# Three stores of 128 rows cut into 114 rows and 14 rows in a one-core attention and MLP gradient kernel

## The chip, the core and the metric

The kernel runs on one core of one Trainium2 chip. The metric is the device time of one execution in microseconds (us); lower is better. A core has a matrix engine (TensorE, PE in the profile), VectorE (DVE), ScalarE (ACT), GpSimd (POOL) and SyncE (SP), which issues the data transfers here, and 16 DMA engines that carry them out between device memory and the core's on-chip memory.

## The reference, cut to what matters

The forward pass adds three things: the input `x`, one decode step of grouped-query attention over a long key/value cache, and a gated MLP without a nonlinearity. The kernel computes this output and the gradients of all tensor inputs that carry one, for a given `grad_out`.

```python
# B=2, Sq=1, D=576, Hq=32, Hkv=16, Sk=4096, Dh=128, F=4608, all bf16
xn  = layernorm(x)
q   = (xn @ wq) per head;  k, v = caches repeated to 32 heads
p   = softmax(q k^T / sqrt(Dh));  o = p v;  A = o @ wo
h   = (xn @ w_gate) * (xn @ w_up);  B_ = h @ w_down
out = x + A + B_
out, vjp = jax.vjp(f, x, k_cache, v_cache, wq, wo, w_gate, w_up, w_down)
return (out, *vjp(grad_out))
```

With two rows of input, nearly all bytes are the caches (each 2x16x4096x128) and the weights, which are read once, and their gradients, which have the same shapes and are written once.

## The kernel before, in words

The work is cut into streams. There are 16 attention steps `s` (8 groups of key/value heads times 2 batch rows); each loads two heads of K and two of V, 1 MB each, transposes them, computes scores, softmax and their gradients, and writes two heads of dK and two of dV, 1 MB each. There are 9 MLP slices of 512 columns, and 8 groups for the projections `wq` and `wo`. Every weight slice is loaded, used, and its gradient (an outer product of a short vector pair) is built in PSUM by PE, copied to on-chip memory by ACT or DVE (the helper `cp`, lines 422 and 424) and stored.

All these streams are generators that ask a planner, `Order`, for engines, buffers and transfers. The planner runs once while the program is built and writes one fixed order of instructions for each engine. It does not run on the chip. Transfers are asked for with `DMA("SP", cost, bytes, row)`, and all of them but two small loads at the start are issued by SP (`nc.sync.dma_start`). The compiler's framework gives every transfer one of eight completion counters in turn, so a transfer is issued only once the transfer eight places before it has landed.

The tiles `big` (16 of 1 MB) hold loaded caches, transposed caches, gate and up weights, and results that wait to be stored (`st`). `put` is the stream of a store. It waits until the result is complete, issues the transfer, and hands its buffer back when the transfer has landed:

```python
def put(dst, src, nbytes, row, tag, slot, ready):
    yield WAIT(*ready)
    for d, x in zip(dst, src):
        yield DMA("SP", 0.36, nbytes, row)
        nc.sync.dma_start(d, x)
    yield ("lrel", tag, slot)
```

`rows_outer` uses it for the gradients of `wo` and `w_down`: 17 slices of 512 rows of 576, laid out as 128 partition rows of 4608 bytes (`row` is 4608 for these and no other store). Each slice is 576 KB. The other stores are dK and dV (rows of 8192 bytes, 1 MB), and the gradients of `wq`, `w_gate` and `w_up` (rows of 1024 to 4096 bytes). The two outputs of two rows each (`rows_put`, line 1422) are stored from the tile `xy`; the second of them is the last transfer in SP's list.

Of the kernel before, what the change touches and what calls it, by code (L numbers as in the profile page):

```python
# [232 lines left out]
def WAIT(*events):  # L233
    return ("wait", events)
# [14 lines left out]
def DMA(engine, cost, nbytes, row=8192):  # L249
    return ("dma", engine, cost, 0.01 + RATE * nbytes / 16e3 * (0.03676 + 8.0 / row))  # L250
# [45 lines left out]
    "wo": [-13, -2, -15, 2, 36, -14, 47, 53],  # L296
    "mlp": [2, 16, -13, 39, 111],
}
LATENCY, DRY, RATE = 0.5, 0.9, 1.009
LM, LAG, DRIFT = 0.67, 2.2, 0.009  # L300
CLK = 1.65
# [9 lines left out]
def kernel(  # L311
# [22 lines left out]
    nc = tc.nc  # L334
# [298 lines left out]
    def dxn(dp, Wm, X, S, pos, xoff, blocks):  # L633
        for s in range(S):
            for q in range(4):
                nc.tensor.matmul(dp[32 * q:32 * q + 32, :], lhsT=view(Wm[:], 0, P, 8 * pos(q, s), [[1, 32]]),  # L636
                                 rhs=view(X, 0, P, xoff(q, s), [[FS, blocks], [2, 32]]),
                                 start=(s == 0), stop=(s == S - 1))

    def put(dst, src, nbytes, row, tag, slot, ready):  # L640
        yield WAIT(*ready)
        for d, x in zip(dst, src):
            yield DMA("SP", 0.36, nbytes, row)
            nc.sync.dma_start(d, x)
        yield ("lrel", tag, slot)

    def unit(mms, pe, cols, ev, done, quad=None, kind="r"):
# [34 lines left out]
    def rows_outer(t, dst, p, event):  # L682
        i = yield ACQ("st")
        st, done = st_t[i], events(FC)
        yield SPAWN(put([dst.rearrange("(p c) n -> p (c n)", c=FC)], [st[:, 0:FC * D]], 128 * FC * D * 2, 4608,
                        "st", i, done), p + pr("store"))
        for j in range(FC):
            yield SPAWN(unit(*rows_unit(j, t, st), done[j]), p)
        yield WAIT(*done)
        yield SET(event)  # L690

    def cols_store(i, dst, width, done):
        return put([dst.rearrange("(c p) n -> p c n", p=P)], [st_t[i][:, 0:4 * width].rearrange("p (c n) -> p c n", n=width)],
                   128 * 4 * width * 2, 2 * width, "st", i, done)
# [25 lines left out]
    def wide_outer(rhss, dst, p, event):  # L720
        width, last = FS * len(rhss), []
        for d0 in (0, 2):
            i = yield ACQ("st")
            done = events(4)
            last += done
            yield SPAWN(put([dst[P * d0:P * d0 + 2 * P, :].rearrange("(c p) n -> p c n", p=P)],
                            [st_t[i][:, 0:2 * width].rearrange("p (c n) -> p c n", n=width)],
                            128 * 2 * width * 2, 2 * width, "st", i, done), p + pr("store"))
            for c in range(2):
                for A in range(2):  # L730
                    yield SPAWN(unit(*wide_unit(rhss, d0 + c, A, st_t[i], c * width), done[2 * c + A]), p)
        yield WAIT(*last)
        yield SET(event)
# [800 lines left out]
```

## Time and profile before

| what | value |
|---|---|
| median of 3 runs | 471.64 us (471.35 to 472.25) |
| the profiled execution: its own time, its span | 471.37 us, 469.6 us |
| PE, DVE, ACT, POOL busy, share of the span | 79%, 79%, 71%, 31% |
| bytes moved | 185.96 MB, mean 396 GB/s |
| mean granted clock of TensorE | 0.710 |

The profiled execution lasts 1.8 us longer than its span from first to last instruction. Times in the views count from the start of the span. A row of the table by stretches gives, for each engine, its busy time and in brackets its instructions, then the granted clock, the mean busy share of the 16 DMA engines (1.00 is all of them all the time; packets that follow each other overlap a little, so it can be over 1), and the rate in GB/s. In the view of the transfers over a stretch, the line `DMA` has the same share in 40 equal slices, in tenths, and the line `GB/s` the rate in each.

### The profile page before, as it was taken

The page shows a single profiled execution, that of the slowest core. Times are in us where ns is not written, and L with a number is a line of the kernel's source. Part 1 is how long each engine was busy: PE and PEld are TensorE (multiplying, and loading weights), DVE is VectorE, ACT ScalarE, POOL GpSimd, SP SyncE. Part 2 cuts the span into 40 slices and gives each one's busy share as a digit, 9 for nine tenths or more (in the row PEclk, how much of TensorE's full clock was granted, in tenths as well). Part 3 has the DMA queues.
Part 4 walks back from the last instruction along what each step waited for, and adds up shares of the span by engine and source line. Part 5 has one row for each costly group of instructions (what it writes and reads, how often), then busy time and mean ns, then how long its engine had stood idle before and what let it go on. Part 6 is the DMA issues. An engine that isn't in the chain of part 4 may idle for free.

```text
span 469.6 us, 15459 instructions
## 1 busy us (share of the span) xinstructions
PE 370.8 (79%) x6636; PEld 217.5 (46%) x6636; DVE 369.5 (79%) x705; ACT 334.3 (71%) x507; POOL 146.8 (31%) x176
## 2 busy tenths in 40 slices
PE   0588688869887777986997669789699898998984
PEld 0455444435653352554463444564345434444453
DVE  9689878967867879688689658978867978898772
ACT  2149668867885948671798638877678678789973
POOL 3350242681330320203252264000843705325100
PEclk9978897767757668776675767956656658566977
DMA  8999999999999999999999999999999989999995
GB/s 317 404 413 403 363 390 419 409 416 421 418 416 420 399 421 406 412 415 419 399 418 404 386 418 424 408 413 342 413 416 393 424 270 416 423 413 413 424 368 176
DMA packets 40053, 185.96 MB, mean 396 GB/s; under 512 B 3496, under 2 KB 11184, under 8 KB 23600
## 3 DMA queue, kind: packets, MB, share of 16 engines
q1 hardware_dynamic: 39976, 184.96, 98.1%
q8 instruction: 52, 0.85, 0.7%
q14 instruction: 17, 0.14, 0.1%
q10 hardware_dynamic: 8, 0.00, 0.0%
HBM read 92.48 MB, written 92.48 MB: 394 GB/s over the span
## 4 chain that ended last, share of the span: by engine, by line
PE 42%; ACT 18%; DVE 18%; DMA 12%; issue 5%; POOL 2%; SPq 2%; ACTq 0%; DVEq 0%; POOLq 0%
ACT big L422 15%; DMA out_dram<-big 10%; DVE big L418 8%; PE ps_m L1378 8%; PE ps_o L1226 7%; PE ps_m L1205 7%; PE ps_o L675 4%; PE ps_m L841 3%; DVE big L424 3%; DMA big<-in_A_v_cache_dram 3%; PE ps_m L967 2%; PE ps_m L636 2%; POOL BD L1193 2%; PE ps_o L712 1%; SPq L1129 1%
## 5 line engine op out<-in xcount | busy, mean ns | idle before, releaser
L422 ACT CAST big<-ps_o 128x1024 bf16<-128x1024 f32 (+4 forms) x319 | 279.7, 950 | 40.3 <-PE ps_o L1226 18.2
L418 DVE STREAM_TRANSPOSE big<-big 128x1024 f32<-128x1024 f32 x146 | 176.1, 1223 | 5.9 <-DMA big<-in_A_v_cache_dram 3.6
L1193 POOL TENSOR_TENSOR BD<-vr,mask 128x2048 bf16<-128x2048 bf16 x32 | 115.2, 3603 | 198.8 <-ACT vr L422 122.2
L424 DVE CAST big<-ps_o 128x1024 bf16<-128x1024 f32 (+2 forms) x71 | 78.2, 1102 | 15.8 <-PE ps_o L675 5.2
L1205 PE MATMUL ps_m<-big,W 128*32 128x128 bf16 x2048 | 57.1, 274 | 5.5 <-ACT osb L422 0.7
L1226 PE MATMUL ps_o<-BD,dd 32*128 32x512 bf16 x256 | 48.8, 489 | 12.7 <-ACT big L422 9.2
L1205 PEld LDWEIGHTS <-W 128*32 128x32 bf16 x2048 | 45.4, 121 | 21.9 <-issue 18.6
L1226 PE MATMUL ps_o<-BD,pp 32*128 32x512 bf16 x256 | 42.1, 461 | 10.4 <-ACT big L422 6.7
L1170 POOL COPY W<-rep 32x16 bf16<-32x16 bf16 x128 | 24.5, 192 | 63.5 <-DVE rep L951 53.2
L418 DVE STREAM_TRANSPOSE big<-ww 128x1152 f32<-128x1152 f32 (+1 forms) x25 | 32.9, 1317 | 4.5 <-DMA out_dram<-big 3.3
L1378 PE MATMUL ps_m<-big,pp 128*32 128x512 bf16 x256 | 28.2, 536 | 1.5 <-DVE small L1330 1.2
L1378 PE MATMUL ps_m<-big,dd 128*32 128x512 bf16 x256 | 27.5, 518 | 1.5 <-DVE dd L418 0.6
L1226 PEld LDWEIGHTS <-dd 32*128 32x128 bf16 x256 | 11.8, 97 | 32.4 <-issue 24.7
L1226 PEld LDWEIGHTS <-pp 32*128 32x128 bf16 x256 | 10.4, 95 | 26.9 <-issue 22.6
L422 ACT CAST osb<-ps_m 128x512 bf16<-128x512 f32 x15 | 8.9, 590 | 15.9 <-PE ps_m L1378 12.6
L675 PE MATMUL ps_o<-dyr,R 32*32 32x288 bf16 x256 | 17.3, 402 | 2.0 <-ACT big L422 2.0
L675 PE MATMUL ps_o<-dyr,hb 32*32 32x288 bf16 x288 | 16.5, 346 | 1.1 <-ACT big L422 0.9
L967 PE MATMUL ps_m<-big,Wdy 128*128 128x128 bf16 x144 | 14.9, 285 | 3.1 <-DVE small L1283 2.0
L712 PEld LDWEIGHTS <-xnr 32*128 32x128 bf16 x368 | 12.5, 119 | 9.3 <-issue 8.6
L422 ACT CAST sp<-ps_m 128x256 bf16<-128x256 f32 x22 | 8.4, 380 | 11.2 <-PE ps_m L1213 11.0
L636 PEld LDWEIGHTS <-wm 128*32 128x32 bf16 x704 | 13.4, 115 | 6.3 <-issue 5.1
L841 PE MATMUL ps_m<-big,Wdy 128*128 128x128 bf16 x162 | 15.6, 272 | 0.6 <-DVE small L1291 0.4
(210 smaller groups left out, 481.9 us busy)
## 6 DMA issues: line engine op xcount, KB each, us to landing
out_dram<-big SPq DMA_DIRECT2D x74, 1024.0 KB, 12.1
big<-in_A_k_cache_dram SPq DMA_DIRECT2D x32, 1024.0 KB, 12.4
big<-in_A_v_cache_dram SPq DMA_DIRECT2D x32, 1024.0 KB, 12.5
out_dram<-big SPq DMA_DIRECT2D x17, 576.0 KB, 11.4
ww<-in_B_w_down_dram SPq DMA_DIRECT2D x9, 576.0 KB, 11.1
ww<-in_A_wo_dram SPq DMA_DIRECT2D x8, 576.0 KB, 11.1
ww<-in_A_wq_dram SPq DMA_DIRECT2D x8, 512.0 KB, 11.6
big<-in_B_w_gate_dram SPq DMA_DIRECT2D x4, 1024.0 KB, 13.1
```

The source lines that it names most:

```text
L418: nc.vector.transpose(out, in_)
L422: nc.scalar.copy(out, in_)
L424: nc.vector.tensor_copy(out=out, in_=in_)
L636: nc.tensor.matmul(dp[32 * q:32 * q + 32, :], lhsT=view(Wm[:], 0, P, 8 * pos(q, s), [[1, 32]]), rhs=view(X, 0, P, xoff(q, s), [[FS, blocks ...
L675: nc.tensor.matmul(o[32 * q:32 * q + 32, aa, 0:HD2], lhsT=view(t, 32 * q, 32, 2 * A + aa, [[4, 32]]), rhs=dyr[32 * q:32 * q + 32, k * HD2: ...
L841: nc.tensor.matmul(dh, lhsT=Wdy[:, e, 2 * k:2 * k + P], rhs=view(X[:], 0, P, 64 * k + e, [[D, FC], [2, 32]]), start=(k == 0 and e == 0), s ...
L967: nc.tensor.matmul(dp, lhsT=Wdy[:, e, 2 * k:2 * k + P], rhs=view(X[:], 0, P, 64 * k + e, [[D, GH], [2, 32]]), start=(k == 0 and e == 0), s ...
L1170: nc.gpsimd.tensor_copy(view(W_t[t][w][:], 32 * a, 32, 6 + 8 * a, [[G * WW, 4], [WW, G], [1, 2]]), view(rep_t[grp[g]["qs"]][:], 32 * a, 32 ...
L1193: nc.gpsimd.tensor_tensor(BD_t[i][:], view(vr_t[v][:], 0, P, 0, [[0, 16], [1, Dh]]), view(mask16[:], 0, P, 0, [[1, 16], [0, Dh]]), ALU.mult)
L1205: nc.tensor.matmul(sc[32 * cq:32 * cq + 32, :], lhsT=view(W[:], 0, P, (be * G + l) * WW + 6 - 4 * c2 - 2 * l, [[1, 32]]), rhs=view(X[:], 0 ...
L1226: nc.tensor.matmul(o[:, k, :], lhsT=pr2[32 * c4:32 * c4 + 32, :], rhs=BD[32 * c4:32 * c4 + 32, 8 * l + 4 * h2:8 * l + 4 * h2 + 4, :], star ...
L1378: nc.tensor.matmul(ct[32 * j:32 * j + 32, :], lhsT=view(rT, 0, P, 4 * c + 2 * l, [[1, 32]]), rhs=kv_t[kvS[s][t][l]][:, Dh * c:Dh * (c + 4) ...
```

## The change

A list `stores` counts the stores with rows of 4608 bytes in the order in which the planner issues them. The 9th, 13th and 15th of the 17 are issued as two transfers, the first 114 partition rows and then the last 14. The planner is asked for one transfer, as before, so its order and its costs are what they were.

```diff
+PARTS, CUT = (114, 14), (9, 13, 15)
...
+    stores = []
+
+    def parted(d, x, parts):
+        if parts is None:
+            nc.sync.dma_start(d, x)
+            return
+        r = 0
+        for n in parts:
+            nc.sync.dma_start(d[r:r + n], x[r:r + n])
+            r += n
+
     def put(dst, src, nbytes, row, tag, slot, ready):
         yield WAIT(*ready)
         for d, x in zip(dst, src):
             yield DMA("SP", 0.36, nbytes, row)
-            nc.sync.dma_start(d, x)
+            if row == 4608:
+                stores.append(slot)
+            parted(d, x, PARTS if row == 4608 and len(stores) in CUT else None)
         yield ("lrel", tag, slot)
```

PE, ACT, DVE and POOL keep their instructions in the same order. SP's list has three transfers more. From the first cut on every transfer takes the next of the eight counters instead of its old one, so it waits for another transfer than before.

## The prediction

> **What bounds the kernel now.** I read the page first, then the stretches of time, then the transfers of the last 5 us, then the waits of SP and the chain.
>
> ```profile
> span 469.6 us, 15459 instructions
> ...
> PE 370.8 (79%) x6636; PEld 217.5 (46%) x6636; DVE 369.5 (79%) x705; ACT 334.3 (71%) x507; POOL 146.8 (31%) x176
> ...
> DMA packets 40053, 185.96 MB, mean 396 GB/s; under 512 B 3496, under 2 KB 11184, under 8 KB 23600
> ...
> q1 hardware_dynamic: 39976, 184.96, 98.1%
> ...
> PE 42%; ACT 18%; DVE 18%; DMA 12%; issue 5%; POOL 2%; SPq 2%; ACTq 0%; DVEq 0%; POOLq 0%
> ```
>
> The 16 DMA engines are busy 98.1% of the span with SP's queue, the compute engines 79% at most. The chain nevertheless puts only 12% on transfers, since it walks back through compute wherever a buffer came free in time. So transfers set the pace, with compute close behind. A mean over 16 engines hides whether they finish together. The end of the span shows that they don't. This is the view of the transfers from 464.4 to 469.6 us, 0.13 us a slice:
>
> ```profile
> DMA  9999998311111000000000000000000000000000
> GB/s 351 366 347 339 331 347 284 97 47 47 47 47 47 32 24 24 24 24 24 24 24 24 24 24 32 24 24 16 24 0 0 0 0 0 0 0 0 0 0 0
> ```
>
> Fourteen engines are done at about 465.4 us. Two go on until 466.1 us (47 GB/s), and one alone until 468.2 us (24 GB/s). So one engine is late: 2.7 us behind fourteen others and 2.0 us behind the second. The kernel's end waits for it. It was late 10 us earlier too. From 457.2 to 458.8 us, SP's queue shows just one engine's worth of packets:
>
> ```profile
> q1 hardware_dynamic: 10, 0.04, 7.5%
> ```
>
> One engine of 16 is 6.25%, and 0.04 MB in 1.6 us is 25 GB/s. While the others had nothing left, this one still worked off its backlog. A transfer has landed only when its last engine is done, so each landing that compute waits for comes when the late engine gets there. The stretches show where the others run dry:
>
> ```profile
> core 0: us, PE busy (x) PEld busy (x) DVE busy (x) ACT busy (x) POOL busy (x), PEclk, DMA share, GB/s
> 100.00:110.00 10.00, 7.36 (x103) 5.17 (x103) 4.48 (x11) 3.70 (x8) 5.96 (x6) 0.50 1.01 423
> 250.00:262.00 12.00, 9.52 (x171) 5.15 (x170) 11.57 (x16) 8.43 (x13) 4.37 (x5) 0.63 0.96 380
> 317.00:330.00 13.00, 11.53 (x209) 5.34 (x212) 10.86 (x19) 9.18 (x14) 0.27 (x1) 0.63 0.96 345
> 345.00:416.00 71.00, 64.41 (x921) 32.78 (x921) 56.98 (x106) 54.35 (x82) 27.02 (x40) 0.62 0.98 391
> 375.00:380.00 5.00, 4.75 (x60) 2.19 (x58) 4.41 (x8) 3.50 (x5) 0.02 (x1) 0.50 0.59 204
> 410.00:415.00 5.00, 5.00 (x104) 3.40 (x108) 3.95 (x7) 4.09 (x7) 0.00 (x0) 0.50 1.02 428
> 455.00:464.00 9.00, 7.29 (x190) 5.13 (x190) 4.92 (x19) 6.40 (x10) 0.00 (x0) 0.88 0.66 235
> ```
>
> With all 16 at work the share is 1.02 (410 to 415). What a row lacks to 1.02, times its length, is the mean idle time of an engine: 0.7 us at 250, 0.8 at 317, 2.8 from 345 to 416 (2.15 of it in the dip from 375 to 380), 3.2 at 455. That is cover for extra work on any engine but the late one.
>
> **How the rows fall on the engines.** SP issues 218 transfers of 64 or 128 rows and two of two rows, ACT two of two rows. The page has 3496 packets under 512 B, and no row of data is that short: 218 x 16 + 4 x 2 = 3496. Each transfer thus ends with one small packet on each engine that it uses: 16 engines for 64 and 128 rows, two for two rows. An equal share per engine fits all three. Carried on, 114 = 6 x 19 uses 6 engines with 19 rows each, and 14 rows use 14 engines with one each. I take these as the same end of the row of engines each time. Then a cut store puts 20 rows on six engines, 1 on eight and 0 on two, where each had 8.
>
> The Trainium skill ("DMA: Bandwidth & Descriptors", "Why a DMA increments its semaphore by 16 and not by 1") gives the rule outright: the largest number up to 16 that divides both sides' row counts, lowest-numbered engines first. The trace agrees for 2, 64 and 128 rows; nothing run so far shows 114.
>
> **The price of a row.** 423 GB/s over 16 engines (100 to 110) is 26.4 GB/s for one, so 4608 bytes take 0.175 us. A cut adds 12 rows or 2.1 us to each of the six, takes 7 rows or 1.2 us from eight, 8 rows or 1.4 us from two. Three cuts: +6.3 us on six, -3.7 and -4.2 us on the rest.
>
> **Where the cuts lie.** SP's timeline, and the size line of the transfers:
>
> ```profile
> 201.69 9.38 SPq L644 DMA_DIRECT2D out_dram<-big  x4
> ...
> 333.61 0.35 SPq L644 DMA_DIRECT2D out_dram<-big  x1
> ...
> 406.66 5.61 SPq L644 DMA_DIRECT2D out_dram<-big  x2
> ```
>
> ```profile
> out_dram<-big SPq DMA_DIRECT2D x17, 576.0 KB, 11.4
> ```
>
> In SP's list the 9th of the 17 is the last of the four at 201.69, the 13th is alone at 333.61, the 15th is the second of the two at 406.66. Issued at about 211, 334 and 412, they land 11.4 us later, at about 222, 345 and 423.
>
> **Is the late engine one of the six?** The end of SP's own wait tells something:
>
> ```profile
> SPq L644 <- ACT big L422: 112.3, 58, 6.9
> ...
> SPq L1087 <- DMA out_dram<-big: 16.0, 10, 3.4
> ...
> SPq L1529 <- DMA out_dram<-big: 3.5, 1, 3.5
> ```
>
> The last wait of the program (L1529) ends with a store of `big`, although the two-row store of `xy` is the last in SP's list. The two engines of that store were done before the late one. If two-row transfers use two of the six, the late engine is one of 14, and four of these are in the six: 4/14, or 0.29, that it is hit, 10/14 that it is relieved. I forecast that it is relieved.
>
> The Trainium skill ("DMA: Bandwidth & Descriptors", "Latency and other measured facts") calls engines 7 and 15 usually slower in traces. With its rule of lowest numbers neither is among the six, which would raise the chance; a view of before doesn't name the engine.
>
> **The sum.** The late engine loses 7 or 8 rows three times: 3.7 to 4.2 us less work, and it has no idle time to lose them in. At the end, fourteen others stand 2.7 us ahead of it and the second latest 2.0 us. If nothing upstream moves, the end comes earlier by 2.0 to 2.7 us. Upstream, three pieces of the chain after the first cut are landings:
>
> ```profile
> 257.52 12.04 DMA big<-in_A_v_cache_dram
> ...
> 300.09 16.17 DMA out_dram<-big
> ...
> 423.19 6.32 DMA out_dram<-big
> ```
>
> The first can end 1.2 us sooner. The third begins just behind the third cut; it can end sooner by 2.4 us (the second and the third cut on the late engine), or later by up to 2.1 us (what the six hold more). So the whole lies between 4.2 us gained and nothing. I take 2.2 us, since the end is shown by rows and the upstream share isn't.
>
> The six: +2.1 us at 222 meet 1.5 us of idle time before 345 (250 and 317), which leaves 0.6. With the next 2.1 they are 2.7 behind and meet 2.8 us (345 to 416), all covered. The last 2.1 meet 3.2 us (455). So they shouldn't end last. Without that cover they would be up to 6.3 us behind.
>
> The smaller edits:
>
> ```profile
> L644 SPq DMA_DIRECT2D out_dram<-big x105: 332/344/2885, 35.3 to 463.5; - x105
> ...
>   ACT big L422: 5.8, 2
>   DVE big L418: 4.3, 3
> ```
>
> Three more issues at 0.34 us are 1.0 us on SP, which waits 112.3 us for ACT's copies. I take zero; at most 1.0 if loads queue behind. The two parts use two of the eight counters, so loads behind them wait for a more recent transfer. Such waits cost 16.0 us in 10 times, 1.6 each. I take zero, since a landing comes some 12 us after its issue and the engines still have work queued; at most 1.6 a cut. A cut store gives its buffer back up to 2.1 us later on the six. ACT and DVE waited 5.8 and 4.3 us in all for buffers of stores, in five places; none is sure to be one of these. Zero to 2.1 us, counted in the range.
>
> The profiled execution took 471.37 us, its span 469.6 us; the median is 471.64 us. 471.37 - 2.2 = 469.2 on the profiled execution, 469.4 us on the median. This case's own range is 467.4 (4.2 gained) to 470.7 us (0.9 gained).
>
> **The rivals.** *The late engine is one of the six.* Then it gets 36 rows more, 6.3 us, and it has no idle time. Every landing that compute waits for comes later, from the first cut on: 471.6 + 6.3 = 477.9 us, and about 475 if half of it falls into stretches where compute sets the pace, as in the dip from 375 to 380. For: 4 of 14 places. Against: 10 of 14. This decides with the first cut: from 222 us on, each landing would be 2.1 us later.
>
> *The six become the late ones.* If their own lateness adds to 2.1 us where the chain waits at 423, that wait ends up to 2.1 us later, and what the end gives is used up: 471.6 to 473.7 us. For it speaks that dips are means over engines, and one of the six can have less. Against it speaks their sum, 7.5 us from 250 to 464 against 6.3 us.
>
> The Trainium skill's rule to use all 16 engines ("DMA: Bandwidth & Descriptors", "Rules for kernel authors") speaks for this rival; no run so far shows it.
>
> *The rows are spread over all engines anyway*, in shares of 7 and 8. Then only three issues are added: 471.7 us.
>
> **How the numbers follow.** A measurement of this kernel can tell about 0.2%, 0.9 us, from no change. Relieved late engine: 0.57 (0.53 faster by more than that, 0.04 within). Late engine hit: 0.27, slower. Six become late: 0.11 (0.03 within, 0.08 slower). Spread anyway: 0.05 (0.04 within, 0.01 slower). Faster 0.53, same 0.11, slower 0.36. The time is that of the likeliest, 469.4 us. The range goes from 467.0 (4.2 us gained, and the runs' own spread of 0.3) to 478.0 us, which takes in the middle of the second case; its upper half stays outside.
>
> **What would show it.** If right, the last 5 us of the changed kernel show the tail of one engine at 24 GB/s shorter than 0.7 us or gone, the 14-row parts are issued right behind the 114-row parts, and the packets under 512 B number 3496 - 48 + 60 = 3508. If instead the tail of one engine grows by several us and dips like those at 375 and 455 get deeper, it was hit. If several engines share a tail of some 2 us, the six are the late ones. If the small packets number 3496 + 48 = 3544, the rows were spread over 16 and the price is wrong.

## The result, and the profile after

| kernel | median us | range, runs |
|---|---|---|
| before | 471.94 | 471.35 to 473.14, 4 |
| three stores as 114 and 14 rows | 478.86 | 477.18 to 479.69, 4 |

The ratio is 1.0144, with a 95% interval from 1.0123 to 1.0165: 6.8 us slower (0.0144 x 471.94). The forecast was 469.4 us. The first rival, "the late engine is one of the six", had 477.9 us. The profiled execution after took 479.12 us with a span of 477.3 us.

The page after, the lines that answer to those of before:

```profile
span 477.3 us, 15459 instructions
...
PE 368.8 (77%) x6636; PEld 215.9 (45%) x6636; DVE 369.6 (77%) x705; ACT 335.1 (70%) x507; POOL 147.1 (31%) x176
...
DMA packets 40065, 185.96 MB, mean 390 GB/s; under 512 B 3508, under 2 KB 11196, under 8 KB 23612
...
q1 hardware_dynamic: 39988, 184.96, 97.5%
...
PE 32%; DMA 26%; DVE 18%; ACT 13%; issue 6%; POOL 2%; SPq 0%; DVEq 0%; ACTq 0%; POOLq 0%
```

Compute has the same busy times (PE 368.8 after 370.8 us, ACT 335.1 after 334.3), so nothing was added there. The share of transfers in the chain went from 12% to 26%; what this share is worth is said with the run of two halves below. The small packets are 3508, as foreseen for six and fourteen engines. The parts were issued one right behind the other in two of the three places; in the second, the two issues took 3.13 us together. This is SP's timeline after:

```profile
212.94 0.85 SPq L651 DMA_DIRECT2D out_dram<-big  x2
...
337.08 3.13 SPq L651 DMA_DIRECT2D out_dram<-big  x2
...
415.50 0.79 SPq L651 DMA_DIRECT2D out_dram<-big  x2
```

The chain after, its transfers from 200 us on:

```profile
208.56 15.10 DMA out_dram<-big
224.06 14.89 DMA ww<-in_A_wo_dram
261.33 11.84 DMA big<-in_A_v_cache_dram
303.81 15.78 DMA out_dram<-big
351.81 13.75 DMA out_dram<-big
403.57 15.14 DMA out_dram<-big
418.79 14.55 DMA big<-in_A_v_cache_dram
```

Before, three transfers stood there with 34.5 us together (12.04, 16.17, 6.32). After, seven stand there with 101.1 us. Two of the four new ones lie near the first cut, but they don't show what it did: the store was issued at 208.56, ahead of the parts (212.94), and the chain of a run that is faster than before (lo4 below) has a landing of 15.26 us at 231.88 too. The rival was to decide with the first cut. That it costs anything is shown by the run with one cut below.

The stretches after, and the last 8 us (0.2 us a slice):

```profile
core 0: us, PE busy (x) PEld busy (x) DVE busy (x) ACT busy (x) POOL busy (x), PEclk, DMA share, GB/s
250.00:262.00 12.00, 9.13 (x118) 4.65 (x121) 10.60 (x16) 10.53 (x15) 2.95 (x10) 0.50 0.91 376
375.00:380.00 5.00, 4.50 (x90) 2.64 (x82) 4.24 (x10) 2.44 (x4) 3.52 (x1) 0.50 1.02 422
422.00:440.00 18.00, 14.48 (x199) 6.32 (x197) 13.98 (x23) 16.85 (x25) 9.41 (x3) 0.62 0.87 307
400.00:477.30 77.30, 61.69 (x984) 33.10 (x983) 53.63 (x102) 57.99 (x84) 16.78 (x9) 0.65 0.89 350
```

```profile
DMA  9997400689999986513711000000000000000000
GB/s 335 356 333 256 149 26 15 236 317 361 346 335 335 361 289 225 179 51 123 251 63 36 20 26 26 20 26 26 26 20 26 26 20 21 0 0 0 0 0 0
```

From 400 us to the end the share was 0.91 before and is 0.89 over a longer time: (1.02 - 0.89) x 77.3 is 10.0 us of mean idle time, against 7.7 us before. The end still is one engine alone with 20 to 26 GB/s, from 473.7 to 476.1 us. That is 2.4 us, little more than the 2.1 us of before. At 470.3 us the same picture shows in the middle of work: 15 to 26 GB/s, one engine.

### The profile page after: what moved, and what is told of

The parts are those of the page before. It is cut to its first block, busy times and chain, and to the rows that moved or that the text cites. A ratio compares the mean times of both kernels' runs of the same rounds, so it can differ in the third digit from the quotient of the medians.

```text
span 477.3 us, 15459 instructions
## 1 busy us (share of the span) xinstructions
PE 368.8 (77%) x6636; PEld 215.9 (45%) x6636; DVE 369.6 (77%) x705; ACT 335.1 (70%) x507; POOL 147.1 (31%) x176
## 2 busy tenths in 40 slices
DMA packets 40065, 185.96 MB, mean 390 GB/s; under 512 B 3508, under 2 KB 11196, under 8 KB 23612
## 4 chain that ended last, share of the span: by engine, by line
PE 32%; DMA 26%; DVE 18%; ACT 13%; issue 6%; POOL 2%; SPq 0%; DVEq 0%; ACTq 0%; POOLq 0%
DMA out_dram<-big 18%; ACT big L425 11%; DVE big L421 9%; DMA big<-in_A_v_cache_dram 6%; PE ps_o L1242 5%; PE ps_m L1221 5%; PE ps_m L1394 5%; DMA ww<-in_A_wo_dram 3%; DVE big L427 3%; PE ps_m L983 3%; PE ps_m L857 2%; PE ps_o L691 2%; POOL BD L1209 2%; PE ps_m L639 1%; PE ps_o L728 1%
## 5 line engine op out<-in xcount | busy, mean ns | idle before, releaser
L1242 PE MATMUL ps_o<-BD,dd 32*128 32x512 bf16 x256 | 48.5, 486 | 15.2 <-ACT big L425 10.8
L1394 PE MATMUL ps_m<-big,pp 128*32 128x512 bf16 x256 | 29.2, 554 | 1.1 <-DVE small L1346 0.7
L691 PE MATMUL ps_o<-dyr,R 32*32 32x288 bf16 x256 | 16.1, 376 | 1.5 <-ACT big L425 1.5
L691 PE MATMUL ps_o<-dyr,hb 32*32 32x288 bf16 x288 | 16.2, 338 | 1.2 <-ACT big L425 1.1
L983 PEld LDWEIGHTS <-Wdy 128*128 128x128 bf16 x144 | 14.2, 134 | 5.6 <-issue 5.6
## 6 DMA issues: line engine op xcount, KB each, us to landing
out_dram<-big SPq DMA_DIRECT2D x74, 1024.0 KB, 13.9
```

What stands on the lines that cost most here:

```text
L691: nc.tensor.matmul(o[32 * q:32 * q + 32, aa, 0:HD2], lhsT=view(t, 32 * q, 32, 2 * A + aa, [[4, 32]]), rhs=dyr[32 * q:32 * q + 32, k * HD2: ...
L983: nc.tensor.matmul(dp, lhsT=Wdy[:, e, 2 * k:2 * k + P], rhs=view(X[:], 0, P, 64 * k + e, [[D, GH], [2, 32]]), start=(k == 0 and e == 0), s ...
L1242: nc.tensor.matmul(o[:, k, :], lhsT=pr2[32 * c4:32 * c4 + 32, :], rhs=BD[32 * c4:32 * c4 + 32, 8 * l + 4 * h2:8 * l + 4 * h2 + 4, :], star ...
L1394: nc.tensor.matmul(ct[32 * j:32 * j + 32, :], lhsT=view(rT, 0, P, 4 * c + 2 * l, [[1, 32]]), rhs=kv_t[kvS[s][t][l]][:, Dh * c:Dh * (c + 4) ...
```

## The experiments

Engines are numbered 0 to 15 here in the order in which transfers of few rows take them. The Trainium skill ("DMA: Bandwidth & Descriptors", "Why a DMA increments its semaphore by 16 and not by 1") has them taken from the lowest number up. The packets of these runs show how many engines each part uses; the number itself no row names. The runs lo2 to lo5 were measured on one chip, the runs from half to lo4x6 on a second one, the last five on two more. On which chip the result above was measured isn't known.

Three explanations were set against each other. A: one engine was late all along, it is one of the six, and it pays 12 rows a cut. B: overloaded engines cost what their overload is, whichever they are. C: the three added transfers cost it, with their issues and counters.

All runs up to the last five change one line, the parts and the stores that are cut. The result of each is given as a ratio to the kernel before on the same chip; below 1 is faster:

| run | parts | stores cut | rows a cut (8 when whole): fullest engines; number 4 | median us | ratio, interval |
|---|---|---|---|---|---|
| lo2 | 34, 80, 14 | 9, 13, 15 | 0 and 1: 23; 6 | 471.97 | 1.0005 (0.9989 to 1.0020) |
| lo3 | 51, 64, 13 | 9, 13, 15 | 0 to 2: 22; 5 | 471.92 | 1.0006 (0.9984 to 1.0028) |
| lo4 | 68, 48, 12 | 9, 13, 15 | 0 to 3: 21; 4 | 470.32 | 0.9967 (0.9951 to 0.9984) |
| lo5 | 85, 32, 11 | 9, 13, 15 | 0 to 4: 20; 20 | 478.35 | 1.0136 (1.0104 to 1.0168) |
| half | 64, 64 | 9, 13, 15 | all: 8; 8 | 472.12 | 1.0006 (0.9989 to 1.0023) |
| one | 114, 14 | 9 | 0 to 5: 20; 20 | 473.70 | 1.0041 (1.0024 to 1.0058) |
| six | 114, 14 | 5, 7, 9, 11, 13, 15 | 0 to 5: 20; 20 | 485.88 | 1.0295 (1.0275 to 1.0316) |
| p120 | 120, 8 | 9, 13, 15 | 0 to 7: 9; 9 | 472.83 | 1.0017 (0.9998 to 1.0036) |
| r2 | 68, 60 | 9, 13 | 0 to 3: 21; 4 | 470.79 | 0.9981 (0.9964 to 0.9998) |
| r3 | 68, 60 | 9, 13, 15 | 0 to 3: 21; 4 | 469.66 | 0.9950 (0.9929 to 0.9970) |
| r3e | 68, 60 | 3, 6, 9 | 0 to 3: 21; 4 | 473.07 | 1.0017 (0.9993 to 1.0041) |
| lo4x6 | 68, 48, 12 | 5, 7, 9, 11, 13, 15 | 0 to 3: 21; 4 | 477.22 | 1.0102 (1.0066 to 1.0138) |

**Which engine: two, three, four or five of them loaded.**

```diff
-PARTS, CUT = (114, 14), (9, 13, 15)
+PARTS, CUT = (34, 80, 14), (9, 13, 15)    # lo2
+PARTS, CUT = (51, 64, 13), (9, 13, 15)    # lo3
+PARTS, CUT = (68, 48, 12), (9, 13, 15)    # lo4
+PARTS, CUT = (85, 32, 11), (9, 13, 15)    # lo5
```

> The same three stores as 34, 80 and 14 rows: 34 rows use two engines with 17 rows each, 80 rows all 16 with 5, 14 rows fourteen with 1. Engines 0 and 1 so carry 23 rows of each cut store (8 before the change), 2 to 13 carry 6, the last two 5. Theory A (one engine was late all along, it is one of the six that the 114-row part uses, but neither 0 nor 1, since a store on two engines alone landed ahead of it): the late engine loses 2 rows a cut, 1.1 us in three; the two loaded ones get 45 rows or 7.9 us more, of which some 4 to 7 us are what they stand ahead of the late one: 471 to 475 us. Theory B (any engines that are overloaded cost what the overload is): 471.9 + 7.9 = 479.8 us. Theory C (it is the added transfers, their issues and counters, not the rows): six more transfers instead of three, twice the 6.9 us of the change: about 486 us.

> The same three stores as 51, 64 and 13 rows: engines 0 to 2 carry 22 rows of each cut store, 3 to 12 carry 5, the last three 4. A: if the late engine is 2, it gets 42 rows or 7.4 us more: 479 us and about the time of the change or over; if it is 3, 4 or 5, it loses 9 rows (1.6 us): 470 to 474 us. B: 471.9 + 7.4 = 479 us, whichever engine is late. C: about 486 us.

> The same three stores as 68, 48 and 12 rows: engines 0 to 3 carry 21 rows of each cut store, 4 to 11 carry 4, the last four 3. A: if the late engine is 2 or 3, it gets 39 rows or 6.8 us more: 479 us; if it is 4 or 5, it loses 12 rows (2.1 us): 470 to 473 us. B: 471.9 + 6.8 = 479 us. C: about 486 us.

> The same three stores as 85, 32 and 11 rows: engines 0 to 4 carry 20 rows of each cut store, 5 to 10 carry 3, the last five 2. A: if the late engine is 2, 3 or 4, it gets 36 rows or 6.3 us more, as in the change: 478 to 479 us; if it is 5, it loses 15 rows (2.6 us): 469 to 473 us. B: 471.9 + 6.3 = 478 us. C: about 486 us. The four runs together: under A there is one step up of 4 to 8 us, at the first of them whose loaded engines include the late one; under B all four are at 478 to 480; under C all four lie above the change.

Two and three loaded engines: no change that could be measured. Four: 1.6 us faster (0.0033 x 471.35). Five: 6.4 us slower. There is one step, between four and five. The step is not one of size, since the fullest engines get 39 rows too many with four of them and 36 with five. Under A the late engine is the fifth to get rows, number 4. B and C fail on the first three runs: 45, 42 and 39 rows too many on other engines and six added transfers cost nothing. From the page the packets, and from the stretches the one with the first cut in it (200 to 300 us), first of the run with four, then of the run with five:

```profile
DMA packets 40101, 185.96 MB, mean 398 GB/s; under 512 B 3544, under 2 KB 11232, under 8 KB 23648
```

```profile
200.00:300.00 100.00, 81.58 (x1437) 49.59 (x1433) 79.58 (x139) 70.04 (x110) 32.09 (x41) 0.68 1.01 410
```

```profile
DMA packets 40101, 185.96 MB, mean 389 GB/s; under 512 B 3544, under 2 KB 11232, under 8 KB 23648
```

```profile
200.00:300.00 100.00, 75.49 (x1408) 44.68 (x1404) 76.53 (x133) 66.91 (x105) 32.08 (x41) 0.73 0.99 399
```

Both have 3496 - 48 + 3 x 32 = 3544 small packets: 4 + 16 + 12 and 5 + 16 + 11 engines. So they have the same number of transfers and packets, and differ in where the rows lie. From 200 to 300 us the rate is 410 GB/s in one and 399 in the other, and compute gets through less there (1408 PE matmuls instead of 1437). The five cost 6.4 us, the whole price of 36 rows (6.3 us at 0.175), so number 4 had nothing to spare, while 0 to 3 had at least the 6.8 us of their 39 rows. What these two runs alone leave is that five loaded engines are one too many, whichever they are; no run loads five others. Against it speaks that the run with four, and r3 below on the second chip, gain by taking rows from engines 4 to 15.

**The added transfers, the dose, and the other end of the row.**

```diff
-PARTS, CUT = (114, 14), (9, 13, 15)
+PARTS, CUT = (64, 64), (9, 13, 15)                # half
+PARTS, CUT = (114, 14), (9,)                      # one
+PARTS, CUT = (114, 14), (5, 7, 9, 11, 13, 15)     # six
+PARTS, CUT = (120, 8), (9, 13, 15)                # p120
```

> The same three stores as 64 and 64 rows: each part uses all 16 engines with 4 rows, so every engine carries 8 rows of a cut store, as before the change; the three added issues and the shifted counters stay. Theories A and B (the rows on the six engines cost the time): 471.9 us, as before the change, within 0.5 us. Theory C (the added transfers, their issues and counters cost it): 478.9 us, as the change.

> Only the 9th of the 17 stores is cut into 114 and 14 rows, the other two stay whole. A (the late engine is among the six and pays 12 rows a cut): a third of the change, 471.9 + 2.1 to 2.3 = 474.1 us. B (the six become late together, after their lead over the late engine is used up): one cut adds 2.1 us to engines that stand several us ahead: 471.9 us or a little less. C: 471.9 + 2.3 = 474.2 us.

> Six of the 17 stores are cut into 114 and 14 rows (5th, 7th, 9th, 11th, 13th, 15th). A: 72 rows more on the late engine, at 0.175 us a row, 12.6 us, or in proportion to the measured 6.9 us of the three cuts 13.8 us: 484.5 to 485.7 us. B: 72 rows less the lead that was used up once (6.3 us of rows cost 6.9, so nothing known of a lead): 484 us or more. C: 485.7 us, with the control of two halves telling it from A.

> The same three stores as 120 and 8 rows: 120 rows use 15 engines with 8 rows each, 8 rows use eight with 1. Engines 0 to 7 carry 9 rows, 8 to 14 carry 8, engine 15 none. A: the late engine, one of the low numbers, gets 3 rows more in all, 0.5 us: 472.4 us, and the relief of engine 15 by 24 rows (4.2 us) brings nothing. If engine 15 were the late one, the time would fall by 2 to 4 us, to 468 to 470. C: 478.9 us.

Two halves cost nothing that could be measured (ratio 1.0006, 0.9989 to 1.0023): three issues and the shifted counters are free within about 1 us, and C is out. One, three and six cuts cost 1.9, 6.8 and 13.9 us, each its ratio less 1 times the median of before. On 12, 36 and 72 rows of the late engine that is 0.16 (0.09 to 0.23 by the interval), 0.19 and 0.19 us a row. The first cut is paid at once, which B excluded. With 120 and 8 rows, the sixteenth engine is relieved of 24 rows and nothing is gained, so it isn't the late one; the 0.8 us (-0.1 to 1.7) that it costs agrees with 3 rows more on number 4 (0.5 us), and with no change. The same stretch from 200 to 300 us, in the order before, half, one cut, three cuts, six cuts:

```profile
200.00:300.00 100.00, 80.30 (x1442) 48.91 (x1442) 78.83 (x137) 69.55 (x111) 32.09 (x41) 0.69 1.01 410
```

```profile
200.00:300.00 100.00, 79.98 (x1431) 48.73 (x1431) 78.97 (x137) 69.56 (x110) 32.17 (x41) 0.69 1.01 408
```

```profile
200.00:300.00 100.00, 77.28 (x1423) 46.30 (x1422) 77.90 (x138) 68.69 (x109) 32.17 (x41) 0.71 1.00 400
```

```profile
200.00:300.00 100.00, 77.09 (x1412) 46.20 (x1411) 76.64 (x137) 67.81 (x106) 32.18 (x41) 0.71 1.00 399
```

```profile
200.00:300.00 100.00, 75.90 (x1340) 46.26 (x1326) 74.30 (x130) 64.36 (x101) 32.16 (x41) 0.66 0.97 388
```

The share hardly moves for one cut (1.01 to 1.00), yet the rate drops from 410 to 399 or 400 GB/s, 2.6%. Over 100 us that is 2.6 us, about what one cut costs. It has the same size with one cut and with three, since just one of the three lies here. Each row is of one execution; two halves, which cost nothing, have 408.

The share of transfers in the chain doesn't sort the runs in this way: it is 18% with two halves, which cost nothing, and 14% with one cut, which costs 1.9 us. Nor does the time from a load's issue to its landing, which differs by some 2 us between kernels of equal time (loads of `wo`: 11.1 us before, 9.0 in lo3, medians). The times and the rate in the stretch do.

**Relieving the late engine.**

```diff
-PARTS, CUT = (114, 14), (9, 13, 15)
+PARTS, CUT = (68, 60), (9, 13)                       # r2
+PARTS, CUT = (68, 60), (9, 13, 15)                   # r3
+PARTS, CUT = (68, 60), (3, 6, 9)                     # r3e
+PARTS, CUT = (68, 48, 12), (5, 7, 9, 11, 13, 15)     # lo4x6
```

> Two stores (9th and 13th) as 68 and 60 rows: 68 rows use four engines with 17 rows each, 60 rows fifteen with 4. Engines 0 to 3 carry 21 rows of each cut store, 4 to 14 carry 4, engine 15 none. Theory A, with the place that the runs with 68 and with 85 rows gave (the late engine is number 4, and only the late one costs time): it loses 8 rows, 1.4 us; engines 0 to 3 get 26 rows, 4.6 us, about what they stand ahead of it: 0.5 to 1.5 us faster than the kernel before, 470.3 to 471.3 us. Theory B (a load that is uneven costs what the fullest engine gets): 4.6 us slower, 476.3 us.

> All three stores of the change as 68 and 60 rows, so one transfer fewer a cut than 68, 48 and 12 rows, and nearly the same rows on each engine (21 on 0 to 3, 4 on 4 to 14, none on 15). A: the late engine loses 12 rows, 2.1 us; engines 0 to 3 get 39 rows, 6.8 us, more than they stand ahead: the same as the three parts, 1.0 us faster than before, 470.8 us. B: 6.8 us slower, 478.6 us.

> 68 and 60 rows at the 3rd, 6th and 9th store, earlier in the kernel. A: the late engine is relieved before more of the landings that compute waits for, and engines 0 to 3 have longer to work their 6.8 us off in stretches where others wait: 1 to 2 us faster than before, 469.8 to 470.8 us. If the lag of the late engine builds up only later, the early cuts make engines 0 to 3 the late ones for a while: 0 to 2 us slower than before. B: 6.8 us slower, 478.6 us.

> Six stores (5th, 7th, 9th, 11th, 13th, 15th) as 68, 48 and 12 rows: engines 0 to 3 get 78 rows or 13.7 us more, the late engine loses 24 or 4.2 us. A: what engines 0 to 3 stand ahead of the late engine (some 4 to 7 us by the runs with 34 and 51 rows, where 7.9 and 7.4 us cost next to nothing) is used up, and they end last: 471.8 + 13.7 less 4 to 7 us: 478.5 to 481.5 us. B (uneven load costs in full): 485.5 us. If not rows but only engine 4 matters: 467.6 us.

With three cuts the kernel is 2.4 us faster than before (0.0050 x 471.94, 1.4 to 3.4 by the interval), at 469.66 us the fastest of all whole kernels; with two cuts it is 0.9 us faster (0.1 to 1.7). B said 6.8 and 4.6 us slower. A had the sign right; with three cuts it had said 1.0 us. The last 8 us of r3, 0.2 us a slice:

```profile
DMA  9999999999999995744573212111111110000000
GB/s 422 335 384 353 371 302 323 343 392 402 343 364 364 381 338 208 256 143 154 179 246 87 77 46 72 51 41 51 51 41 51 51 42 10 0 0 0 0 0 0
```

No engine is alone any more: two end together (41 to 51 GB/s), after three or four (72 to 87 GB/s). The tail of one engine has gone. That the loaded engines have caught up with it fits, but no row names who ends last; in lo4, with nearly the same rows on the other chip, one engine still ends alone, for some 1.8 us. That is the end of what can be moved this way: with six cuts engines 0 to 3 get 13.7 us more, the late one 4.2 us less, and the kernel is 4.8 us slower (3.1 to 6.5; expected were 6.7 to 9.7). So 13.7 - 4.8 = 8.9 us of the load on these four was covered, by what they stood ahead and by their idle time together. With the cuts earlier (3, 6 and 9) nothing is gained, 0.8 us slower with an interval that holds no change. This agrees with a lag that builds up only later. That the position decides was the second of the two expectations for this run; no run here separates it further.

**The transfers by themselves.** All else is left out, arithmetic, other outputs, and with them the kernel's order. Sources are cleared tiles.

```python
for n in range(64):                # 1 MB each: both caches, 32 heads of the two rows
    if LOADS:                      # ld, mix
        nc.sync.dma_start(got[n % 8], cache[n])
    if STORES:                     # st, mix; st4, st5: parts for n = 16 and 32
        moved(grad[n], big[n % 8], PARTS if n in CUT else (128,))
```

> All that is left of the kernel are 64 stores of 1 MB (128 rows of 8192 bytes, 8 on each engine, the gradients of both caches, as zeros); loads, arithmetic and the other outputs are left out. 512 rows of 8192 bytes on each engine at 26.4 GB/s are 159 us, plus some 10 us of filling and start. Theory D (stores take longer on number 4, and its lag builds up with them): one engine ends alone, 2 to 15 us behind the others, with 24 to 26 GB/s in that time. Theory E (the lag comes from loads, or from the mix with other traffic): all 16 end within 1 us.

> All that is left are 64 loads of 1 MB of both caches, and no output is written. D: no engine ends alone, all are done within 1 us. E with loads: one engine ends alone, 2 to 15 us behind. Each load waits for the one eight places before it, so a late engine shows here as a lower rate of all as well.

> The 64 stores alone, two of them cut into 68 and 60 rows: engines 0 to 3 get 26 rows of 8192 bytes more (8.1 us at 26.4 GB/s), 4 to 14 get 8 fewer (2.5 us), 15 gets 16 fewer. D: number 4 ends 2.5 us earlier, and so does the program if its lag in the stores alone is over 8 to 10 us; with a smaller lag engines 0 to 3 end last. E: engines 0 to 3 end last together, about 8 us later than the stores alone.

> The 64 stores alone, two of them cut into 85, 32 and 11 rows: engines 0 to 4 get 24 rows more (7.4 us), the others 10 or 12 fewer. D: number 4 ends 7.4 us later than in the stores alone, by itself, whatever its lag. E: engines 0 to 4 end last together, 7.4 us later than the stores alone. Against the run with 68 and 60 rows: D says slower by 9.9 us if the lag is large, E the same within 1 us.

> 64 loads and 64 stores of 1 MB in turn, no arithmetic, no other output: 1024 rows of 8192 bytes on each engine, 318 us at 26.4 GB/s and some 10 us of filling and start. Theory F (loads beside stores make one engine late): at the end one engine works alone for 2 to 10 us. Theory G (it needs the rest of the kernel): all 16 are done within 1 us, as in the stores alone and the loads alone.

Medians: 168.62 us (stores), 164.88 us (loads), 184.77 us (stores, two as 68 and 60), 185.11 us (two as 85, 32 and 11), 322.06 us (loads and stores in turn). The last 5 us of the stores alone, of the loads alone, and of both in turn, 0.125 us a slice:

```profile
DMA  9694994948949499494794949946100000000000
```

```profile
DMA  9999799999999979999999994770000000000000
```

```profile
DMA  4969999697994979919194040310300000000000
```

In the first two, all engines stop within about 0.5 us. In the third the end thins out over some 1.3 us, more than the 1 us that G allowed. In none does one engine work alone for 2 us or more. So D (stores make an engine late), E with loads, and F (the mix makes it late) fail: on these two chips no engine is late by itself. Which engine is late in the whole kernel there was not measured. What of the rest of the kernel makes one late isn't settled; neither the other shapes of transfers nor the fetching of instructions was tried in a run.

The traces hold a hint for the second. The page of before counts packets of instructions beside those of data, where each of the five programs of transfers has at most one:

```profile
q8 instruction: 52, 0.85, 0.7%
q14 instruction: 17, 0.14, 0.1%
```

From 457.2 to 458.8 us, where only the late engine works on data, one of each kind passes:

```profile
q8 instruction: 1, 0.02, 3.4%
q14 instruction: 1, 0.01, 1.8%
```

By the single packets of that trace, one of the 52 (16 KB each) takes 0.96 us (median), and in that time one data packet fewer is under way than just before it (15.2 against 16.2, medians). Behind 51 of the 52, within 0.12 us of the end, starts a row of data that takes over 1.7 times its usual time, 0.40 us too long (median). Some 3 or 4 us away from them that is so in about one case of ten. So each holds up one engine by some 1.4 us, as an estimate from these two times, and two more of them on one engine than on another would be a lag of 2.7 us. Whether number 4 gets more of them than the others isn't shown.

The cuts in the stores alone also missed every number. Both cost 16 us, with four or five engines loaded. That fits with no engine being special there (E). But E said 8.1 and 7.4 us, half of it. The page's spans and queues, stores alone, then with 68 and 60 rows:

```profile
span 166.7 us, 118 instructions
...
q1 hardware_dynamic: 9216, 67.11, 97.2%
```

```profile
span 183.0 us, 120 instructions
...
q1 hardware_dynamic: 9222, 67.11, 90.7%
```

The same bytes took 0.972 x 166.7 = 162.0 us of an engine's time before and 0.907 x 183.0 = 166.0 us after, 4.0 us more on the mean of 16, or 64 us in all. The rates of the run with 68 and 60 rows show when, 4.6 us a slice:

```profile
GB/s 0 372 423 412 424 419 414 424 417 406 328 349 419 417 426 423 419 426 372 365 378 340 301 426 421 419 428 419 419 423 417 417 423 419 417 421 295 107 95 27
```

Behind each cut the rate falls from some 420 GB/s to 301 to 378, from 46 to 55 and from 82 to 105 us. That is some 5.5 us lost for all engines, beside the 8.1 us by which four are loaded. The rest lies at the end, where four engines' worth (107 and 95 GB/s) is followed by one engine's (27). By the single packets, 217 of the 8192 rows took 0.44 us or more (median 0.62, where 0.31 is usual), all between 44.9 and 103.0 us; in the stores alone none did. Why rows behind a cut take twice as long here isn't shown.

## Why the prediction was wrong

**The step that failed is the place of the late engine** ("Is the late engine one of the six?"). It gave 4 of 14 to the case that it is hit, and took the other. It is hit: three cuts cost 6.8 us, about the price of 36 rows on it (6.3 us), where the forecast had it lose 7 or 8 rows a cut. On the chip of lo2 to lo5 it is the fifth engine, number 4. The argument from the two-row store left engines 2 to 15 in question, and the runs agree with that. But it left them equal, and the choice among 14 places was a guess with no row behind it. The Trainium skill's sentence on engines 7 and 15 ("DMA: Bandwidth & Descriptors", "Latency and other measured facts") was to raise the chance of the forecast. The same row of it gives a best guess at the cause, which it calls specific to transfers described by GpSimd (SWDGE); the prediction left that out, and the transfers here are issued by SP, in the queue `q1 hardware_dynamic`. The measurements differ, too: with 85, 32 and 11 rows both are relieved, by 15 and 18 rows, and the kernel is 6.4 us slower.

**The mechanism held on both sides.** One engine is late and has no idle time. Rows added to it cost about their price from the first cut on. Rows taken from it gain: the forecast's 2.2 us, meant for this change, is close to what r3 gives (2.4 us), which takes 4 rows from it in each of three stores instead of 7 or 8. That the two sizes are so near is in part luck, since r3's interval goes from 1.4 to 3.4 us.

**The price of a row** was 0.175 us. The runs with one, three and six cuts show 0.16 to 0.19. The rival's 477.9 us was 1.0 us under the measured 478.86; its 6.3 us stand against 6.8. Part of it may be that transfers lasted longer: 0.981 x 469.6 = 460.7 us of an engine's time before, 0.975 x 477.3 = 465.4 after, with the same bytes.

**How rows fall on engines** held in each run of the whole kernel, by the small packets: 3508 for three cuts, and 3544 for both runs shown above (lo2 has one more than it should, 3545, but not in SP's queue). The rival that rows are spread over all engines is out.

**The six as a group**: for engines 0 to 3 an extra load of 6.8 us was covered, as the prediction said of 6.3 us; number 5 was not tested by itself. For these four the cover was 8.9 us, more than the 7.5 us of mean idle time; what they stand ahead of the late engine may be the rest. The second rival's mechanism fits the run with six cuts of 68, 48 and 12 rows (4.8 us slower).

**The smaller edits** were taken at zero: half shows 0.3 us (-0.5 to 1.1). SP still waits above all for copies, and ahead of the loads of line 1103 (1087 before) for stores no more than before; ahead of stores for earlier stores it waits 12.7 us instead of 3.8. Its waits after:

```profile
SPq L647 <- ACT big L425: 104.6, 54, 6.8
...
SPq L1103 <- DMA out_dram<-big: 16.4, 11, 2.4
```

They were 112.3 and 16.0 us.

**What would show it** was wrong in one point. If the late engine was hit, its tail was to grow by several us. It has 2.4 us instead of 2.1. The length of the tail doesn't sort the runs: with two halves, which cost nothing, one engine works alone for 3.4 us (20 to 26 GB/s). This is its rate over the last 8 us, 0.2 us a slice:

```profile
GB/s 351 346 371 246 169 128 67 41 164 190 46 95 254 28 23 23 35 26 26 26 20 26 26 20 26 26 20 26 26 26 20 26 26 20 0 0 0 0 0 0
```

A reading that fits, and isn't shown, is that a late engine that holds up each landing holds up compute, and so the issue of everything behind it: its delay is passed on to all, and the end looks as it did. The sign was to be looked for in the rate of the stretch with the first cut in it (410 to 399 GB/s). Of the two dips that were named, neither is where it was: from 375 to 380 the share is 1.02, from 455 to 464 it is 1.01. One now stands at 422 to 440 (0.87, against 1.03), behind the third cut.

## What to carry to other kernels

A mean busy share of 16 engines doesn't say whether they are in step; look at the last microseconds and at any dry spell for the rate of one engine alone. If one is late, a change of shape that moves a few rows costs or gains by what lands on that one, and up to several us on the others are free. Its place can't be had from such a view, so before a chance is put on it, find it with runs that load two, three, four and five engines.

## What the runs showed of the hardware

- On one chip (lo2 to lo5) the late engine is the fifth to get rows. On a second one it is the fifth or the sixth: among the six by the run with one cut, not among the first four by the gain of r3. On two further chips, in 64 MB of stores, 64 MB of loads, and both in turn, no engine is late by 2 us.
- 26 rows of 8192 bytes too many on four engines cost 16 us in a stream of stores alone, not the 8.1 us at 26.4 GB/s, where 217 rows behind the cuts took 0.62 instead of 0.31 us; 36 to 72 rows of 4608 bytes on the late engine of the whole kernel cost 0.19 us each, near their plain price.
- 39 to 45 rows too many on engines that aren't late cost nothing that could be measured in 472 us, with up to six more transfers.
- A 16 KB packet of instructions takes 0.96 us, about one data packet fewer is under way in that time (15.2 instead of 16.2), and behind 51 of 52 of them a row takes 0.40 us too long (the kernel before).
